# The last three output tiles: two copy engines and three DMA queues in place of one of each

## The chip, the cores and the metric

The kernel runs on one core of one Trainium2 chip. The metric is the device time of one execution in microseconds (us). A core has a matrix engine (PE, with PEld for its weight loads), a vector engine (DVE), a scalar engine (ACT), a general engine (POOL, called `gpsimd` in the code) and a queue engine (SP, `sync` in the code). SP, ACT and POOL can each start a DMA transfer. Each engine works through its own list of instructions in order; engines wait for one another by counting semaphores.

## The reference

Three layers run one after the other on 2304 tokens of 512 features.

```
ret  = (scale * q @ k^T) * decay_mask @ v            # 4 batches x 8 heads, 576 positions
x    = ret as (2304, 512)
x    = sum over the top 2 of 8 experts: weight * relu(x @ w1[e]) @ w2[e]
h    = x @ w_in                                      # (2304, 512) @ (512, 2048)
g    = h * clip(h + 3, 0, 6) / 6
out  = g @ w_out                                     # (2304, 512)
```

The change stands at the very end of the last product: where finished tiles of `out` leave the chip's on-core memory.

## The kernel before

Everything is float32; a product of the expert layers and of the last layer is made of three passes over high and low parts. `run` (L966) calls `attention`, `moe`, `moe2` and `rest` in that order.

`moe2` takes the 18 row tiles of 128 tokens in seven groups (`GR`): three groups of two tiles, then four of three. For each group, 16 steps of the hidden dimension (f = 0 to 15) are made: `g1` (L639) fills a PSUM tile `ga` or `gb`, `glu` (L814 to L817) applies the activation on ACT and DVE, and `g2` (L650) adds this step's part to the group's accumulators, one PSUM tile `p` of 128x512 for each row tile. `g2` runs one step late, through `flush`: the products of step f stand behind the `g1` of step f+1, so that PE need not wait for the activation. In `g2` the accumulators are finished one after the other: in the last step all products of the first, then of the second, then of the third.

When a group's last step is flushed, `o_out` copies each accumulator from PSUM to a row tile `s` on ACT (L824) and sends it to `out` from SP's queue (L825). For all groups but the last, this lies beside the next group's products. The last group, tiles 15 to 17, has nothing behind it.

Behind `moe2` stands `rest` (L868 to L872). It is for an uneven routing of tokens: each engine loads a count that was stored in the tile `more` early in the program (at 147.0 us) (`values_load`, L870), and skips the body when the count is zero (the `If`, L871). With this input it is zero, so all five engines jump over `rest_body`:

```
        most = nc.values_load(self.more[0:1, 8:9], min_val=0, max_val=MORE)
        with tc.If(most > 0):
            self.rest_body()
```

Behind the jump each engine has a few semaphore instructions that stand under L871; POOL has there one `INC_SWDGE_SEM`, which sets the counts of its DMA queue. Then comes the end of the tile context, whose instructions carry L1010: SP waits in turn for the counts of all DMA queues and engines, POOL has a `DRAIN` without any wait, and then all engines meet in a barrier that POOL collects and releases.

Of the kernel before, what the change touches and what calls it, by code (L numbers as in the profile page):

```python
# [12 lines left out]
AF = mybir.ActivationFunctionType  # L13
# [6 lines left out]
NT = N // 128  # L20
# [12 lines left out]
P = 128  # L33
# [31 lines left out]
class K:  # L65
# [754 lines left out]
    def o_out(self, t0, acc):  # L820
        nc = self.nc
        for j, a in enumerate(acc):
            o = self.row([P, DM])
            nc.scalar.activation(o, a, AF.Copy)  # L824
            nc.sync.dma_start(self.out[(t0 + j) * P:(t0 + j + 1) * P, :], o)  # L825

    def count(self):
# [185 lines left out]
```

## Time and profile before

| what | value |
|---|---|
| time, median of 3 runs | 1013.08 us (1012.91 to 1014.62) |
| the profiled execution's own time | 1017.49 us |
| span of the profiled execution, first to last instruction | 1015.7 us |
| PE busy | 982.1 us, 97% of the span |
| ACT, DVE, POOL busy | 411.0, 524.1, 190.8 us |
| mean granted TensorE clock | 0.989 |

The profiled execution is a single one with the profiler on; its own time lies 4.4 us above the median of the runs, and its span 1.8 us below its own time. All times inside the program are counted from the span's start. The end of the span is the end of the last instruction of any engine.

### The profile page before, as it was taken

How to read it: one execution, taken by the hardware profiler on the slowest of the kernel's cores; microseconds unless marked ns; L12 is line 12 of the kernel's file. 1: busy time of each engine (PE TensorE's matmuls, PEld its weight loads, DVE VectorE, ACT ScalarE, POOL GpSimd, SP SyncE). 2: the span in 40 equal slices, each digit the busy share in tenths (PEclk: the TensorE clock that was granted, in tenths of full speed). 3: DMA queues.
4: the chain of work that ended last, by engine and by line, in shares of the span. 5: the costliest groups of instructions: out<-in, count | busy, mean ns of one | idle time of the engine just before them, and what ended most of it. 6: DMA issues, size and time to landing. Idle time of an engine off the chain costs nothing.

```text
span 1015.7 us, 16598 instructions
## 1 busy us (share of the span) xinstructions
PE 982.1 (97%) x6268; PEld 876.9 (86%) x6268; DVE 524.1 (52%) x1264; ACT 411.0 (40%) x845; POOL 190.8 (19%) x257
## 2 busy tenths in 40 slices
PE   7999798999999999999999999999999999999996
PEld 5888687989888898988898889999999999999995
DVE  4679563767675767767664366333423333233221
ACT  3557423544334343533433365433333333333322
POOL 0043352023322332332320113011010100000000
PEclk9999899999999999999999999999999999999999
DMA  9998637744757366474525553111010110000000
GB/s 179 226 287 237 208 145 234 262 153 129 244 160 246 120 225 192 128 241 153 192 74 168 159 180 120 49 32 52 22 42 21 53 42 1 32 1 1 32 1 34
DMA packets 130921, 128.97 MB, mean 127 GB/s; under 512 B 66065, under 2 KB 94993, under 8 KB 130833
## 3 DMA queue, kind: packets, MB, share of 16 engines
q1 hardware_dynamic: 124432, 106.85, 35.5%
q0 software_dynamic: 6400, 20.98, 6.1%
q8 instruction: 51, 0.84, 0.3%
q14 instruction: 38, 0.30, 0.1%
HBM read 92.80 MB, written 35.00 MB: 126 GB/s over the span
## 4 chain that ended last, share of the span: by engine, by line
PE 86%; DMA 7%; DVE 2%; SPq 1%; ACT 1%; POOL 1%; issue 1%; another core or an unknown queue 0%; DVEq 0%; POOLq 0%; ACTq 0%
PE p L650 37%; PE ga L639 20%; PE gb L639 18%; DMA yd<-s 3%; PE xp L612 2%; PE px L218 2%; PE sc L196 2%; PE px L208 1%; PE p L179 1%; DMA s<-in_moe_w_out_dram 1%; DMA s<-in_moe_w_in_dram 1%; SPq L161 1%; PE p L256 1%; PE p L241 1%; POOL xe L377 1%
## 5 line engine op out<-in xcount | busy, mean ns | idle before, releaser
L650 PE MATMUL p<-b,h 128*128 128x512 f32 (+1 forms) x1824 | 452.1, 393 | 0.0
L650 PEld LDWEIGHTS p<-b,h 128*128 128x128 f32 (+1 forms) x1824 | 330.7, 186 | 65.3 <-DVE h L817 0.3
L639 PE MATMUL ga<-x,b 128*128 128x360 f32 (+2 forms) x1344 | 235.0, 324 | 0.8 <-ACT x L613 0.8
L639 PEld LDWEIGHTS ga<-x,b 128*128 128x128 f32 x1344 | 217.7, 189 | 7.8 <-ACT x L613 1.0
L639 PE MATMUL gb<-x,b 128*128 128x384 f32 (+2 forms) x768 | 129.5, 317 | 0.0
L639 PEld LDWEIGHTS gb<-x,b 128*128 128x128 f32 x768 | 121.0, 188 | 4.0
L583 POOL TENSOR_TENSOR cvl<-cvl,cva 128x256 f32<-128x256 f32 x64 | 48.8, 762 | 258.0 <-ACT h L692 113.3
L542 DVE TENSOR_TENSOR b<-b,b 128x512 fp32r<-128x512 f32 x128 | 89.6, 737 | 12.1 <-ACT b L541 8.5
L639 PE MATMUL gb<-b,b 128*128 128x256 f32 x672 | 89.8, 283 | 0.0
L817 DVE SCALAR_TENSOR_TENSOR h<-h,h 128x384 fp32r<-128x384 f32 (+1 forms) x112 | 56.2, 501 | 61.1 <-ACT h L816 61.1
L639 PEld LDWEIGHTS gb<-b,b 128*128 128x128 f32 x672 | 87.2, 192 | 0.4
L757 POOL DMA_INDIRECT s<-yd,slotc x36 | 34.8, 968 | 262.7 <-DVE s L766 81.8
L816 ACT ACTIVATE h<-h 128x384 fp32r<-128x384 f32 (+1 forms) x112 | 53.6, 479 | 63.6 <-DVE h L815 62.1
L541 ACT ACTIVATE b<-b 128x512 fp32r<-128x512 f32 x128 | 74.5, 625 | 11.7 <-PE p L650 11.6
L815 DVE SCALAR_TENSOR_TENSOR h<-h,ga 128x384 f32<-128x384 f32 (+1 forms) x56 | 27.8, 497 | 94.3 <-ACT h L814 94.0
L815 DVE SCALAR_TENSOR_TENSOR h<-h,gb 128x384 f32<-128x384 f32 (+1 forms) x56 | 27.8, 497 | 93.4 <-ACT h L814 93.3
L814 ACT ACTIVATE h<-ga,three 128x384 f32<-128x384 f32 (+1 forms) x56 | 30.0, 535 | 97.9 <-PE ga L639 94.6
L814 ACT ACTIVATE h<-gb,three 128x384 f32<-128x384 f32 (+1 forms) x56 | 30.0, 536 | 87.9 <-PE gb L639 86.1
L692 ACT ACTIVATE h<-ga 128x360 fp32r<-128x360 f32 (+1 forms) x64 | 29.4, 459 | 73.1 <-PE ga L639 61.4
L584 POOL TENSOR_TENSOR cvl<-cvt,cvl 128x256 f32<-128x256 f32 x64 | 56.7, 885 | 5.0
L693 DVE SCALAR_TENSOR_TENSOR h<-gb,h 128x256 fp32r<-128x256 f32 (+1 forms) x64 | 27.7, 433 | 53.8 <-PE p L650 33.6
L692 ACT ACTIVATE h<-gb 128x256 fp32r<-128x256 f32 (+1 forms) x64 | 25.3, 395 | 67.5 <-PE gb L639 67.3
(134 smaller groups left out, 871.0 us busy)
## 6 DMA issues: line engine op xcount, KB each, us to landing
b<-in_moe_w_dram SPq DMA_DIRECT2D x64, 512.0 KB
s<-in_moe_w_in_dram SPq DMA_DIRECT2D x32, 256.0 KB
s<-in_moe_w_out_dram SPq DMA_DIRECT2D x32, 256.0 KB
s<-xe SPq DMA_DIRECT2D x24, 240.0 KB
yd<-s SPq DMA_DIRECT2D x24, 240.0 KB
out_dram<-s SPq DMA_DIRECT2D x18, 256.0 KB
b<-in_k_dram SPq DMA_DIRECT2D x16, 256.0 KB
b<-in_q_dram SPq DMA_DIRECT2D x16, 256.0 KB
```

The costliest lines, as they stand in the source:

```text
L541: self.nc.scalar.activation(h, a, AF.Copy)
L542: self.nc.vector.tensor_sub(l, a, h.bitcast(F32))
L583: nc.gpsimd.tensor_mul(lf, lf, a.bitcast(F32))
L584: nc.gpsimd.tensor_add(lf, t.bitcast(F32), lf)
L639: nc.tensor.matmul(p, a[:, k, f], b[:, k, :n], start=(i == 0), stop=(i == 11))
L650: nc.tensor.matmul(a[:R], x[:, c], y[:, fi, :], start=(first and i == 0), stop=(last and i == 2))
L692: nc.scalar.activation(hh, p, AF.Relu)
L757: nc.gpsimd.indirect_dma_start(out=r, out_offset=None, in_=self.yd[0:rows], in_offset=bass.IndirectOffsetOnAxis(ap=self.slotc[:, t, k:k + ...
L814: nc.scalar.activation(r, p, AF.Relu, bias=self.three)
L815: nc.vector.scalar_tensor_tensor(r, r, 6.0, p, op0=OP.min, op1=OP.mult)
L816: nc.scalar.activation(gh, r, AF.Copy, scale=1.0 / 6.0)
L817: nc.vector.scalar_tensor_tensor(gl, r, 1.0 / 6.0, gh.bitcast(F32), op0=OP.mult, op1=OP.subtract)
```

## The change

In the last group (`last`), the first and the third accumulator are copied by ACT as before and the second by DVE. The three sends are issued by SP, POOL and ACT in this order, where SP issued all three. All other groups keep ACT and SP.

```diff
         for j, a in enumerate(acc):
             o = self.row([P, DM])
-            nc.scalar.activation(o, a, AF.Copy)
-            nc.sync.dma_start(self.out[(t0 + j) * P:(t0 + j + 1) * P, :], o)
+            last = t0 + len(acc) == NT
+            if last and j == 1:
+                nc.vector.tensor_copy(o, a)
+            else:
+                nc.scalar.activation(o, a, AF.Copy)
+
+            q = (nc.sync, nc.gpsimd, nc.scalar)[j] if last else nc.sync
+            q.dma_start(self.out[(t0 + j) * P:(t0 + j + 1) * P, :], o)
```

The change adds six lines ahead of `rest`, so that L870, L871 and L1010 of before are L876, L877 and L1016 of after.

SP, the end of its list ahead of the skipped body: the last three sends of `out`, the load of the count, a check of its range (ISA), and the jump. Before:

```order
L825 DMA out_dram<-s_10527 128x512
L825 DMA out_dram<-s_10530 128x512
L825 DMA out_dram<-s_10533 128x512
L870 TENSOR_LOAD more
L870 ISA x2
L871 COMPARE_AND_BRANCH
L906 DMA sd<-slots 128x18x2
```

And now:

```order
L831 DMA out_dram<-s_10527 128x512
L876 TENSOR_LOAD more
L876 ISA x2
L877 COMPARE_AND_BRANCH
L912 DMA sd<-slots 128x18x2
```

Two sends have left SP's list (`L906`, or `L912`, is the first row of the skipped body). The count is now loaded behind the first send of the three, not behind the third.

POOL, the same place: its last rows before were gathers of tokens for the last group, issued long before the end of the program. Before:

```order
L757 DMA s_9721<-yd,slotc 128x512
L757 DMA s_9848<-yd,slotc 128x512
L757 DMA s_9850<-yd,slotc 128x512
L870 TENSOR_LOAD more
L871 COMPARE_AND_BRANCH
```

And now:

```order
L757 DMA s_9848<-yd,slotc 128x512
L757 DMA s_9850<-yd,slotc 128x512
L831 DMA out_dram<-s_10530 128x512
L876 TENSOR_LOAD more
L877 COMPARE_AND_BRANCH
```

The send of the second tile stands between POOL's last gather and its load of the count; the load, the jump and all that follows the jump on POOL are behind that send, which waits for DVE's copy. In the same way DVE has its copy ahead of its load of the count, and ACT has one copy less and a send of the third tile ahead of its own.

## Rows read from the trace of the kernel before

**Rows 1.** The page: busy PE, the clock in 40 slices, the ended chain by engine.

```profile
PE 982.1 (97%) x6268; PEld 876.9 (86%) x6268; DVE 524.1 (52%) x1264; ACT 411.0 (40%) x845; POOL 190.8 (19%) x257
PEclk9999899999999999999999999999999999999999
PE 86%; DMA 7%; DVE 2%; SPq 1%; ACT 1%; POOL 1%; issue 1%; another core or an unknown queue 0%; DVEq 0%; POOLq 0%; ACTq 0%
```

**Rows 2.** Four stretches: busy us (instructions) by engine, clock, DMA share, GB/s.

```profile
core 0: us, PE busy (x) PEld busy (x) DVE busy (x) ACT busy (x) POOL busy (x), PEclk, DMA share, GB/s
943.00:1003.00 60.00, 60.00 (x305) 54.80 (x304) 15.58 (x28) 16.15 (x30) 0.00 (x0) 1.00 0.04 14
1003.00:1007.30 4.30, 4.27 (x18) 2.85 (x17) 1.11 (x2) 2.30 (x4) 0.00 (x0) 1.00 0.03 6
1007.30:1015.70 8.40, 0.00 (x0) 0.00 (x0) 0.00 (x0) 0.60 (x1) 0.00 (x0) 0.73 0.28 100
```

**Rows 3.** Order of time, from 1005.5 us: start, length, engine, line.

```profile
1005.12 2.15 PE L650 MATMUL p<-b,h 128*128 128x512 f32 x8
...
1005.92 1.98 ACT L824 ACTIVATE s<-p 128x512 f32<-128x512 f32 x3 [1.19 <-PE p L650]
1006.54 2.54 SPq L825 DMA_DIRECT2D out_dram<-s  x3
```

**Rows 4.** L825, the last three sends: ns min/median/max, first and last start.

```profile
L825 SPq DMA_DIRECT2D out_dram<-s x3: 332/383/1367, 1006.5 to 1008.7; - x3
```

**Rows 5.** L870, L871 and L1010 on SP: the load, the jump, the closing waits.

```profile
L870 SPq TENSOR_LOAD <-more x1: 685/685/685, 1009.1 to 1009.1; - x1
...
L871 SPq COMPARE_BRANCH  x1: 50/50/50, 1010.2 to 1010.2; - x1
L871 SPq EVENT_SEMAPHORE  x9: 17/17/17, 1013.4 to 1014.0; - x9
...
L1010 SPq DRAIN  x3: 7/7/13, 1014.8 to 1015.1; - x3
```

**Rows 6.** L870 and L871 on ACT, DVE and PE's weight loader.

```profile
L870 ACTq TENSOR_LOAD <-more x1: 732/732/732, 1007.3 to 1007.3; - x1
L871 ACTq COMPARE_BRANCH  x1: 50/50/50, 1008.1 to 1008.1; - x1
L871 ACTq EVENT_SEMAPHORE  x2: 17/17/17, 1010.6 to 1010.7; - x2
...
L870 DVEq TENSOR_LOAD <-more x1: 546/546/546, 1004.8 to 1004.8; - x1
L871 DVEq COMPARE_BRANCH  x1: 72/72/72, 1005.4 to 1005.4; - x1
L871 DVEq EVENT_SEMAPHORE  x2: 21/21/21, 1008.5 to 1008.6; - x2
...
L871 PEldq COMPARE_BRANCH  x1: 3822/3822/3822, 1006.0 to 1006.0; - x1
```

**Rows 7.** L870, L871 and L1010 on POOL.

```profile
L870 POOLq TENSOR_LOAD <-more x1: 501/501/501, 832.0 to 832.0; - x1
L871 POOLq COMPARE_BRANCH  x1: 53/53/53, 832.6 to 832.6; - x1
L871 POOLq EVENT_SEMAPHORE  x3: 17/17/17, 835.4 to 835.6; - x3
L871 POOLq INC_SWDGE_SEM  x1: 1784/1784/1784, 835.7 to 835.7; - x1
L1010 POOLq DRAIN  x3: 44/107/6600, 837.5 to 1015.4; - x3
L1010 POOLq EVENT_SEMAPHORE  x4: 17/17/17, 1014.9 to 1015.6; - x4
```

**Rows 8.** L757, POOL's gathers from 828 us on; DMA in 831 to 836 us, 40 slices.

```profile
L757 POOL DMA_INDIRECT s<-yd,slotc x2: 944/944/944, 828.7 to 832.2; - x2
...
DMA  8976100000000000000000199573889200000000
```

**Rows 9.** POOL's drain at the program's start (L998).

```profile
L998 POOLq DRAIN  x1: 198/198/198, 0.3 to 0.3; - x1
```

**Rows 10.** Copies and products of one 128x512 float32 tile on DVE.

```profile
L198 DVE TENSOR_TENSOR b<-sc,cst x36: 678/682/692, 9.4 to 119.1; 128x512 f32<-128x512 f32 x36
L624 DVE TENSOR_SCALAR s<-s x40: 415/419/428, 122.7 to 558.3; 120x512 f32<-120x512 f32 x24, 128x512 f32<-128x512 f32 x16
```

**Rows 11.** DMA from 1010 to 1014 us in 40 slices of 0.1 us.

```profile
DMA  9999691111140200000000000000000000000002
```

## Prediction

> **What bounds the kernel now.** I read the page first. PE is busy for 97% of the span, the granted clock is full in nearly every slice, and the chain that ended last is PE for 86% [rows 1]. The reader is to see there that over the whole run PE sets the time, and then to put that aside: the change touches no product, and the only PE work beside it ends before it matters. The stretches show this. From 943 to 1003 us PE is busy without a gap; from 1007.3 us to the end of the span, 8.4 us, PE is not busy at all and ACT for 0.60 us [rows 2]. So 8.4 us at the end belong to neither products nor copies, and the change can only move what lies in them.
>
> The order of time shows what the compute engines still do: PE's last products end at 1007.3, ACT's three copies run from 1005.92 to 1007.90, SP issues three sends from 1006.54 to 1009.08 [rows 3]. The third copy starts when the third accumulator is done, at 1007.3, so ACT follows PE and isn't late. The rest of the tail is sequencer work that no busy share counts, so I read it line by line. SP issues the sends (0.33, 1.37 and 0.38 us for one) [rows 4], loads the count at 1009.1, jumps at 1010.2, executes its next instruction only at 1013.4, 3.2 us later, goes through its closing waits until 1014.9, and 0.8 us of barrier later the span ends at 1015.7 [rows 5, 7]. The gap behind the jump is on every engine: 2.5 us on ACT, 3.0 on DVE, 3.8 within the branch on PE [rows 6], 2.8 on POOL [rows 7]. SP comes to its jump last, so SP sets the end. The last packets of `out` have moved by 1011.4 [rows 11], before SP even begins to wait for their counts: the sends themselves don't set the end.
>
> POOL has done its whole ending 170 us earlier: count at 832.0, jump at 832.6, next instruction at 835.4, the queue's count set at 835.7 (1.78 us), and then a drain that starts at 837.5 and takes 6.6 us, until 844.1. From the count's load to the drain's end that is 12.1 us, all hidden now [rows 7].
>
> **The change, part by part.** The sums are made against the profiled execution (span 1015.7, own time 1017.49 us) and carried as a difference to the median of 1013.08, which lies 4.4 us below it.
>
> *ACT loses a copy (0.60 us) and gets a send.* The third copy waits for PE until 1007.3 either way, so the lost copy is worth nothing; the other engine's copy lies beside it. The send must wait for the copy's end at 1007.9. No ACT send is in the trace; by SP's rows it takes 0.33 to 1.37 us. I take 0.33. Behind it ACT needs 3.4 us from the load of its count to its last semaphore (1007.3 to 1010.7) [rows 6], which makes 1011.6, or 1012.7 with the long issue. SP's closing waits ask for ACT's count near their end, at about 1012.5, so the long issue is just at the edge and the short one hidden.
>
> *SP loses two sends.* Its first send ends at 1006.9; its load of the count then stands at 1006.9 in place of 1009.1. Everything behind it on SP comes 2.2 us sooner, its last wait at 1012.7 in place of 1014.9. The bounds of this gain: 2.2 us if nothing else is late, nothing if another engine arrives at the barrier at 1014.9 or later.
>
> *DVE gets a copy.* The second accumulator is ready near 1006.6, when ACT began its second copy. The nearest rows are a DVE product from PSUM, 0.68 us, and a DVE operation within on-core memory, 0.42 us [rows 10]; I take 0.7, since the first reads PSUM too. The copy ends at 1007.3. DVE's own ending takes 3.8 us from the load of its count to its last semaphore [rows 6]; it is over by about 1010.5 and hidden by SP.
>
> *POOL gets a send.* This is the term that decides. The send waits for DVE's copy, so POOL's sequencer stands there until 1007.3, and the load of the count, the jump, `INC_SWDGE_SEM` and the drain are all queued behind it in POOL's list. The issue itself costs no more than before: in the trace POOL's last gather (0.94 us, from 832.2) [rows 8] runs while the load and the jump already go on beside it [rows 7], so I start the 12.1 us at 1007.3. That gives: jump at 1007.9, next instruction 1010.7, drain from 1012.8 to 1019.4. [...] The data of POOL's send is not in this sum: the packets of the last gather had moved by 835.0 [rows 8], 2.8 us after its issue, so POOL's send is in by about 1010.5.
>
> The unknown is the length of the drain. Rows give it between 0.04 us and 6.6 us: two POOL drains at the very end take 0.04 and 0.11 us [rows 7], one at the program's start 0.20 us [rows 9], and the one in just this place, behind the gathers and `INC_SWDGE_SEM`, 6.6 us. The change leaves its place and what stands ahead of it in the list alike, and adds one more transfer of POOL's kind, so I take 6.6. Nor was it waiting for data: the last packets were 2.5 us past when it began [rows 8]. With the lower bound the drain ends at 1013.0 and the span at 1013.8, **−1.9 us**. The jump on POOL may take longer than 2.8 us, since now all five engines jump within some 2 us: up to PE's 3.8, which adds up to 1.0.
>
> On the route of a send, the row has SP's issues at 2.5 us in all, of which 2.2 go. The Trainium skill (DMA: Bandwidth & Descriptors, "Issuing engines are not separate DMA queues") says that starting DMAs on several engines saves only the time that the sequencer takes to initiate them. By this page alone the sum would be −2.2 us; by the rows it is −2.2 on SP and +6.7 (1019.4 against 1012.7) on POOL. The same page ("SWDGE vs HWDGE vs iDMA") advises that plain transfers go to SP or ACT, without a price; the trace of before has no plain one on POOL.
>
> **The rivals.** *A: the drain is short* (0.2 us). Then POOL is ready at 1013.0, SP at 1012.7, and the span is 1.9 us shorter: 1011.2. For it: every other drain of POOL is that short, and the long one may belong to the busy stretch around 840 us rather than to its place. Against it: it is the only drain that has DMA work ahead of it. The point that decides is a drain of 2.1 us: from there POOL is at the barrier no sooner than SP was at 1014.9, and the gain is gone; from 4.1 us on the kernel is slower by more than 0.2%. The Trainium skill's sentence on several engines, above, would lead to nearly this time.
>
> *B: the drain is there, but partly paid off*, ending between 1014 and 1017: 1012 to 1015, no change that can be told. That needs a drain of 1 to 4 us, of which no row has an example.
>
> *C: POOL is later still*: a first plain send on POOL costs more than a gather, or the jumps hinder one another for more than the 1.0 us allowed above: 1019 to 1020. Against it: POOL's jump at 832.6 already was one of a program in full work.
>
> **How the numbers follow.** Forecast (drain of 6.6 us): 0.62; A: 0.20; B: 0.12; C: 0.06. The predicted time is 1013.08 + 4.5 = **1017.6 us**. The forecast's own range is 1016.6 to 1019.0, from the spread of the runs before (1012.91 to 1014.62) and the 1.0 us of the jump. The range that holds eight in ten has to take in A, so it goes from 1011.0 to 1019.3. A difference of 0.2%, 2.0 us, is about what a measurement can tell here. Slower takes the forecast, C and some of B: 0.69. Same takes A, whose −1.9 us is just short of the bound, and most of B: 0.27. Faster is left with the edge of A: 0.04.
>
> **What the changed profile would show.** The load of the count on SP at 1006.9 and SP's last closing wait at about 1012.7; DVE's copy of 0.7 us from 1006.6; on POOL the count's load at about 1007.3, the jump 0.6 us later, a drain that begins near 1012.8 and ends near 1019.4; the barrier behind it and nothing else busy. The span would be 1020.2. I'm wrong if POOL's drain there is under 4 us, or if the end is set by an engine other than POOL; everything ahead of 1005 us should stand as it was.

## The result, and the profile after

The changed kernel takes 1021.7 us (median of 7 runs, 1020.01 to 1028.44), the kernel before 1014.38 us (7 runs, 1012.91 to 1016.67). The ratio is 1.008, with a 95% interval of 1.0057 to 1.0102: slower by 6 to 10 us. The direction was forecast, the size was not: 1017.6 us was predicted, with a range up to 1019.3.

The profiled execution has a span of 1022.3 us against 1015.7, 6.6 us longer. All but 0.1 us of it lies behind the last product. The order of time from 1005.5 us on (start, length, engine, line; in brackets the idle time ahead of it and what ended it) answers to [rows 3]:

```profile
1005.27 2.12 PE L650 MATMUL p<-b,h 128*128 128x512 f32 x8
...
1006.06 0.60 ACT L828 ACTIVATE s<-p 128x512 f32<-128x512 f32 x1 [1.18 <-PE p L650]
1006.68 0.33 SPq L831 DMA_DIRECT2D out_dram<-s  x1
1006.75 0.69 DVE L826 COPY s<-p 128x512 f32<-128x512 f32 x1 [1.28 <-PE p L650]
1007.43 0.60 ACT L828 ACTIVATE s<-p 128x512 f32<-128x512 f32 x1 [0.78 <-PE p L650]
1007.74 0.60 POOL L831 DMA_DIRECT2D out_dram<-s  x1 [174.42 <-DVE s L826]
1008.06 0.38 ACTq L831 DMA_DIRECT2D out_dram<-s  x1
```

The copies and sends do what the change says, each on its engine, and the last send is issued at 1008.4 in place of 1009.1. PE's products end some 0.1 us later than before, which is no effect of the change. POOL had stood idle for 174 us until DVE's copy released it; that bracket is the change in one number.

What follows on POOL answers to [rows 7], line by line (lines 876, 877 and 1016 are 870, 871 and 1010 of before):

```profile
L876 POOLq TENSOR_LOAD <-more x1: 522/522/522, 1007.7 to 1007.7; - x1
L877 POOLq COMPARE_BRANCH  x1: 53/53/53, 1008.3 to 1008.3; - x1
L877 POOLq EVENT_SEMAPHORE  x3: 17/17/17, 1012.6 to 1012.8; - x3
L877 POOLq INC_SWDGE_SEM  x1: 1813/1813/1813, 1012.9 to 1012.9; - x1
L1016 POOLq DRAIN  x3: 44/113/6690, 1014.8 to 1022.0; - x3
L1016 POOLq EVENT_SEMAPHORE  x4: 17/17/17, 1021.5 to 1022.2; - x4
```

SP answers to [rows 5]:

```profile
L876 SPq TENSOR_LOAD <-more x1: 523/523/523, 1007.1 to 1007.1; - x1
L877 SPq COMPARE_BRANCH  x1: 50/50/50, 1008.0 to 1008.0; - x1
L877 SPq EVENT_SEMAPHORE  x9: 17/17/17, 1010.8 to 1012.5; - x9
L1016 SPq EVENT_SEMAPHORE  x14: 17/28/2016, 1012.6 to 1022.2; - x14
L1016 SPq DRAIN  x3: 7/7/13, 1015.3 to 1021.7; - x3
```

SP has its count 2.0 us sooner, as the change makes it. That gain is lost again. SP's nine semaphore instructions behind the jump take 1.7 us from first to last, where they took 0.6 before; why is not shown. One of its closing waits lasts 2.0 us (the 2016 ns), over a count of POOL's queue that POOL's `INC_SWDGE_SEM` sets only at 1014.7: this wait ends 0.06 us ahead of that instruction's end here and in e2, e7 and e10 below. SP is through at 1015.4, and stands 6 us more for POOL's drain.

### The profile page after: what moved, and what is told of

Same layout as the page of the kernel before. It is cut to its first block, busy times and chain, and to the rows that moved or that the text cites. A ratio compares the mean times of both kernels' runs of the same rounds, so it can differ in the third digit from the quotient of the medians.

```text
span 1022.3 us, 16598 instructions
## 1 busy us (share of the span) xinstructions
PE 981.6 (96%) x6268; PEld 876.5 (86%) x6268; DVE 525.7 (51%) x1265; ACT 410.6 (40%) x844; POOL 192.0 (19%) x258
## 4 chain that ended last, share of the span: by engine, by line
PE 66%; issue 21%; DMA 6%; DVE 2%; POOL 1%; SPq 1%; ACT 1%; POOLq 0%; DVEq 0%; ACTq 0%
PE p L650 27%; PE ga L639 16%; PE gb L639 13%; PE xp L612 2%; DMA s<-in_moe_w_out_dram 2%; PE px L218 2%; DMA s<-xe 1%; PE px L208 1%; PE sc L196 1%; DMA yd<-s 1%; PE p L179 1%; SPq L161 1%; PE p L256 1%; PE p L241 1%; POOL xe L377 1%
## 5 line engine op out<-in xcount | busy, mean ns | idle before, releaser
L757 POOL DMA_INDIRECT s<-yd,slotc x36 | 35.0, 971 | 262.6 <-DVE s L766 81.8
```

Source lines behind the costliest of these rows:

```text
L757: nc.gpsimd.indirect_dma_start(out=r, out_offset=None, in_=self.yd[0:rows], in_offset=bass.IndirectOffsetOnAxis(ap=self.slotc[:, t, k:k + ...
```

## The experiments

Theory P: the loss is POOL's ending, which the send moves from 832 us to behind the last tiles. Theory Q: sending from several queues costs, and POOL's drain only fills a wait. All ratios are to the kernel before, run on the same chip beside them (its medians there were 1009.1 to 1009.3 us). "Tail" is the time from the start of the last product to the end of the span: 8.83 us before, 15.28 us in the changed kernel. It leaves out the spread of the work ahead of it. But each tail comes from one execution: e4 below, whose last group does the same as the kernel before, has 8.00 us, so a difference of under 1 us between two tails tells nothing.

**e1_no_pool**, the changed kernel without its POOL send:

```diff
-            q = (nc.sync, nc.gpsimd, nc.scalar)[j] if last else nc.sync
+            q = (nc.sync, nc.sync, nc.scalar)[j] if last else nc.sync
```

> The changed kernel with its second send moved from POOL to SP; copies and ACT's send stay. Theory P (the loss is POOL's ending, moved behind the last tiles): the whole loss goes. SP's second send is issued near 1007.5 us and takes 0.33 to 1.37 us, its count's load stands near 1008 in place of 1009.1, so the span ends 0.3 to 1.3 us earlier than before: ratio to before 0.998 to 1.000. Theory Q (the loss comes from sending from several queues, ACT's first send or transfers that meet, and POOL's long drain only fills the wait): still slower by 3 us or more, ratio 1.003 and up.

Measured: ratio 0.9992 (0.998 to 1.0004), tail 8.46 us. The loss is gone, with DVE's copy and ACT's send still there. That is what P forecast; Q falls.

**e2_pool_alone**, the kernel before with one POOL send:

```diff
-            nc.sync.dma_start(self.out[(t0 + j) * P:(t0 + j + 1) * P, :], o)
+            q = nc.gpsimd if t0 + j == NT - 2 else nc.sync
+            q.dma_start(self.out[(t0 + j) * P:(t0 + j + 1) * P, :], o)
```

> The kernel before, with only the second of its last three sends moved from SP to POOL; all copies on ACT. Theory P: the same loss as the whole change. POOL is released near 1007.3 us by ACT's second copy, its drain starts between 1012.8 and 1014.8 and takes 6.6 us, and the span is 4.5 to 7 us longer: ratio 1.0045 to 1.007. Theory Q: without ACT's send and DVE's copy less than half of it, under 3 us.

Measured: ratio 1.0059 (1.0042 to 1.0076), tail 15.72 us. The POOL send alone makes the whole loss.

**e3_pool_touch**, one POOL instruction on one element, no POOL send:

```diff
             nc.sync.dma_start(self.out[(t0 + j) * P:(t0 + j + 1) * P, :], o)
+            if t0 + j == NT - 2:
+                nc.gpsimd.tensor_copy(self.spacer, o[0:1, 0:1])
```

> The kernel before, with one added POOL instruction and no POOL send: POOL copies one element of the second of the last three tiles once ACT has copied it, into a tile that nothing reads. Theory P1 (the drain of 6.6 us belongs to POOL's ending, whatever stood ahead of it): POOL's ending moves behind 1007.3 us as in the changed kernel, drain of about 6.6 us, 4.5 to 6.5 us slower, ratio 1.0045 to 1.0065. Theory P2 (the drain waits for a DMA that POOL issued some us ahead of it): the last gather is then 170 us past, the drain takes 0.2 us or less, POOL meets the barrier near 1013 to 1014.5, before SP, and the time is that of before within 0.2%.

Measured: ratio 1.0061 (1.0042 to 1.0081), tail 13.76 us. So it need not be a send: a copy of one element on POOL is enough. POOL's lines there (its copy is over at 1000.5 us):

```profile
L873 POOLq COMPARE_BRANCH  x1: 53/53/53, 1001.2 to 1001.2; - x1
L873 POOLq EVENT_SEMAPHORE  x3: 17/17/17, 1004.2 to 1004.4; - x3
L873 POOLq INC_SWDGE_SEM  x1: 1772/1772/1772, 1004.5 to 1004.5; - x1
...
L1012 POOLq DRAIN  x3: 44/107/6600, 1006.3 to 1013.4; - x3
```

The last gather of POOL had landed 178 us before, and the drain still takes 6.60 us. P2, that it waits for a transfer, falls.

**e4_pool_early**, a POOL send in the last group but one (as e2, with `NT - 5`):

> The kernel before, with one send moved to POOL, but in the last group but one (tiles 12 to 14, its second tile, near 943 us); the last three sends stay on SP. Theories P1 and P2: POOL's ending moves to 943 to 957 us, with its drain of about 6.6 us, and is hidden by 50 us of the last group's work: the same time as before within 0.2%. A rival, that a plain send from POOL is dear in itself wherever it stands (descriptors written by POOL, a queue that it shares with the gathers): slower by more than 2 us here too.

Measured: ratio 0.9992 (0.9979 to 1.0004), tail 8.00 us. The send is there, the ending with its drain of 6.69 us stands at 942.5 us beside 57 us of products, and costs nothing:

```profile
L1011 POOLq DRAIN  x3: 44/113/6690, 942.5 to 1007.3; - x3
```

**e5_act_two**, the three sends on SP, ACT and ACT:

```diff
-            q = (nc.sync, nc.gpsimd, nc.scalar)[j] if last else nc.sync
+            q = (nc.sync, nc.scalar, nc.scalar)[j] if last else nc.sync
```

> The changed kernel with its second send moved from POOL to ACT, so that SP sends one tile, ACT two, POOL none. Theory P (POOL's ending was the whole loss and SP's list sets the end otherwise): SP's load of the count stands 2.2 us sooner than before, as in the changed kernel, ACT's ending at about 5.7 us after the last matmul's start is just hidden, the tail from the last matmul's start to the end shrinks from 8.8 to 6.6 to 7.2 us: ratio 0.9978 to 0.9985. Rival: ACT's two sends make ACT the last at the barrier, and nothing is gained: ratio 0.9995 or more.

Measured: 1007.39 us against 1009.28, ratio 0.9982 (0.9973 to 0.9992), tail 6.86 us. This version is faster than the kernel before, and by the two ratios than the changed kernel too. SP's lines show why: the count at 1000.7 us, 0.05 us after the last product's start (2.26 before), and the last closing wait 6.0 us after it (8.0 before). Of this, 0.7 us are a wait for ACT's count (the 685 ns): the wait that the rival named is there, but too short to take the gain.

```profile
L876 SPq TENSOR_LOAD <-more x1: 519/519/519, 1000.7 to 1000.7; - x1
...
L1016 SPq EVENT_SEMAPHORE  x14: 17/28/685, 1005.2 to 1007.4; - x14
L1016 SPq DRAIN  x3: 7/7/13, 1006.6 to 1006.9; - x3
```

**e7_pool_late**, the changed kernel with POOL delayed:

```diff
+            if last and j == 1:
+                z = self.row([P, DM])
+                for _ in range(4):
+                    nc.gpsimd.tensor_copy(z, o)
             q.dma_start(self.out[(t0 + j) * P:(t0 + j + 1) * P, :], o)
```

> The changed kernel, with four copies of the second output tile on POOL (into a tile that nothing reads) ahead of POOL's send, so that POOL jumps some us after the other four engines. Theory J1 (POOL's jump took 4.3 us in the changed kernel and 2.9 before because all engines fetch code then): 2.6 to 3.4 us here, and the drain again 6.6 to 6.7 us. Theory J2 (a send of its own in flight makes POOL's jump long): 4 us or more here too. The time itself is longer than the changed kernel's by the copies, some 3 to 6 us.

Measured, in a single execution (1016.67 us, too few for a ratio): the drain 6.69 us, tail 16.53 us, and POOL's jump:

```profile
L881 POOLq COMPARE_BRANCH  x1: 53/53/53, 1001.7 to 1001.7; - x1
L881 POOLq EVENT_SEMAPHORE  x3: 17/17/17, 1005.2 to 1005.4; - x3
```

That is 3.5 us, between what J1 and J2 gave. The copies took 0.6 us each, less than I had reckoned, so POOL jumps only 1.4 us after ACT and the engines are not quite apart.

**e8_before_no_rest** and **e9_after_no_rest**, both kernels without the overflow path:

```diff
             self.moe2()
-            self.rest()
```

> The kernel before without the call of its overflow path behind the last layer (left out: the load of the count, the jump and the body that this input skips). Theory: SP goes from its third send, over at 2.2 us after the last matmul's start, straight to its closing waits and stands there until the third send's data are in, near 4.8 us; with 0.8 us of barrier the tail is about 6 us in place of 8.8, ratio 0.997. POOL's drain, now without INC_SWDGE_SEM ahead of it, tells whether that instruction makes it long: 6.6 us if it belongs to the end of the program, 0.2 us or less if it belongs to INC_SWDGE_SEM.

> The changed kernel without the overflow path (left out as in the run before it). If the drain of 6.6 us belongs to the end of the program: it starts within 1 us of POOL's send, near 1.5 us after the last matmul's start, ends near 8.1, tail about 9 us, so 3 us slower than the kernel before without that path and near the unshortened kernel before, ratio 0.999 to 1.001. If it belongs to INC_SWDGE_SEM: the drain is short, the tail about 5.5 us, ratio 0.9965.

Measured: e8 0.9964 (0.9952 to 0.9975), tail 4.25 us; e9 1.0011 (1.0001 to 1.0021), tail 8.82 us. The load of the count and the jump cost the kernel before 4.6 us of tail, more than I had taken (2.8); by the ratio it is 3.6 us. Some of it lies in the sends: SP's are over 1.4 us after the last product's start, 2.2 before, since the second takes 0.33 us here and took 1.37, and the last of SP's waits for their data ends 3.1 us after it, where I had taken 4.8. Why the second send is shorter is not shown. Between e8 and e9 there are 4.6 us of tail, again POOL's drain. It stands here without `INC_SWDGE_SEM`; in e8, behind the last gather:

```profile
L1009 POOLq DRAIN  x3: 40/102/7783, 825.0 to 1003.9; - x3
```

And in e9, behind the send:

```profile
L1015 POOLq DRAIN  x3: 40/108/7328, 999.4 to 1007.2; - x3
```

These records begin as the gather or the send ahead of them is taken up; counted from the end of that one, the drain is again 6.6 to 6.7 us. So it doesn't belong to `INC_SWDGE_SEM`.

**e10_early_drain_send**, the changed kernel with one drain more on POOL, behind its last gather:

```diff
                 self.x2_prep(gi + 1, f - 1)
+                if gi == len(self.GR) - 1 and f == 4:
+                    self.nc.gpsimd.drain()
```

> The changed kernel with one added POOL drain behind the last gather, near 833 us, hidden by the last group's products. Theory D1 (the long drain clears something that has piled up since the program's start, and only the first drain behind much work is long): the added drain takes 6.6 us, the closing one 0.2 us or less, POOL meets the barrier near 7.9 us after the last matmul's start, and the time is near that of before, ratio 0.999 to 1.001. Theory D2 (a POOL send or INC_SWDGE_SEM just ahead makes a drain long): the closing drain takes 6.6 us again, ratio 1.006 to 1.008, like the changed kernel.

Measured: 1008.75 us, ratio 0.9996 (0.9983 to 1.001), tail 7.51 us. The loss is gone with the POOL send still in place:

```profile
L808 POOLq DRAIN  x1: 7782/7782/7782, 824.3 to 824.3; - x1
...
L879 POOLq COMPARE_BRANCH  x1: 58/58/58, 1000.5 to 1000.5; - x1
L879 POOLq EVENT_SEMAPHORE  x3: 17/17/17, 1004.7 to 1004.9; - x3
L879 POOLq INC_SWDGE_SEM  x1: 203/203/203, 1005.0 to 1005.0; - x1
...
L1018 POOLq DRAIN  x3: 50/113/141, 1005.2 to 1006.4; - x3
```

The added drain at 824.3 us took the 6.6 us (and 1.2 us beside the gather), hidden by products. The closing one, in the same place behind the send and `INC_SWDGE_SEM`, takes 0.14 us, and `INC_SWDGE_SEM` 0.20 us in place of 1.81.

**e11_early_drain_touch**, the same drain added to e3:

> The kernel before with POOL's copy of one element of the last tile but one, no POOL send, and the added POOL drain behind the last gather. D1: the closing drain takes 0.2 us or less, time as before, ratio 0.999 to 1.001. D2 in its part on INC_SWDGE_SEM: the closing drain takes 6.6 us, ratio 1.0045 to 1.0065; if only a send makes it long, 0.2 us here and 6.6 us in the run with the send. A third, D3: a POOL drain takes 6.6 us at each place but right behind another one or at the program's start; then it is 6.6 us in both runs, as in D2.

Measured: ratio 1.0011 (0.9996 to 1.0026), tail 8.18 us, and the longest closing drain 0.107 us:

```profile
L875 POOLq INC_SWDGE_SEM  x1: 167/167/167, 1005.6 to 1005.6; - x1
...
L1014 POOLq DRAIN  x3: 38/41/107, 1005.8 to 1008.8; - x3
```

What D1 forecast came in both, and D2 and D3 fall: the drain is long only where much POOL work has passed since the last one. The lengths of the drains say more about what piles up. POOL issues 80 transfers in the kernel before:

```profile
xe<-s,slots POOLq DMA_INDIRECT x36
s<-yd,slotc POOLq DMA_INDIRECT x36
...
xe<-s,free POOLq DMA_INDIRECT x8
```

Behind these 80 the drain takes 6.60 us, also with e3's copy added. Behind 80 and a plain send it takes 6.69 us (the changed kernel, e2, e4, and e7 with its four copies). With e10's early drain only the one send lies ahead of the closing drain, 0.141 us, and in e11 only a copy, 0.041 us. So a send adds 0.09 to 0.10 us wherever it stands and copies add nothing, and 6.56 us over 80 transfers are 0.082 us for each. This last figure is an estimate: no run has another number of gathers, and what POOL's other work of those 800 us adds is not told apart.

**e6_copies_only**, the changed kernel's copies with `q = nc.sync`:

> The changed kernel's copies (ACT, DVE, ACT) with all three sends on SP. The third copy starts when the third accumulator is ready, as before, and SP's second send when the second copy is, some 0.1 us later since DVE's copy takes 0.69 us against 0.60: no change within 0.1%, ratio 0.999 to 1.001. A rival, that freeing ACT of one copy shortens the tail: 0.6 us, ratio 0.9994, which this measurement can hardly tell; the tail in the trace can.

Measured: ratio 1.0 (0.9986 to 1.0014), tail 9.08 us. The split of the copies alone gains nothing.

## Why the prediction was right in its mechanism and wrong in its size

**POOL gets a send, and its whole ending stands behind it.** Right. SP, ACT and DVE are through by 1015.4, 1012.3 and 1010.8 us, and POOL's drain ends at 1021.5. e1, e2 and e4 show that the POOL send at the end is the cause, and the only one.

**The drain takes 6.6 us again, not 0.2.** Right: 6.69 us, and rival A, a short drain, did not come. Rival B, a drain of 1 to 4 us, did not come either. Of the reason I gave, that its place and what stands ahead of it stay alike, only the second half holds: in e10 the drain has the same place and takes 0.14 us. What it is can be said better now: it is the first drain after POOL's work, and its length goes with the transfers that POOL has issued since the last one. The three short drains that I had as a lower bound [rows 7, 9] fit this: one comes at the program's start, ahead of all transfers, and two come behind a long one.

**POOL's ending takes 12.1 us from 1007.3.** This is the term that was mis-sized. It took 13.7 us (1007.7 to 1021.5), and began 0.4 us late. Nearly all of the 1.6 us is the jump: 4.3 us, where 2.8 were taken and 3.8 allowed. The bound of 1.0 us was PE's jump of 3.8, and no reason was given why POOL's should stay within it. Rival C, at 0.06, allowed for a jump longer by more than 1.0 us, and that came (1.5); its other half, that a plain send costs more to issue than a gather, did not (0.60 us against 0.94). Over the runs POOL's jump, from the branch's end to the next instruction, was:

| POOL's instruction just ahead | no other engine's jump beside it, or little | the other engines' jumps beside it |
|---|---|---|
| a gather | 2.5 to 2.8 (before, e1, e5, e6) | no run |
| a copy of one element | no run | 3.0 (e3), 3.2 (e11) |
| a plain send | 3.3 (e4), 3.5 (e7) | 4.3 (changed), 4.7 (e2), 4.2 (e10) |

Each number is from one profiled execution. The three of over 4 us have both, a send just ahead and the others' jumps beside them. But more of the others' jumps lies beside these three (8.4 to 9.7 us, added up over the four engines) than beside those of e3 and e11 (5.5 and 5.7 us), so how much the send does and how much the other jumps do is not told apart: J1 and J2 both stay open. The Trainium skill (Runtime: NRT & Kernel Launch, "Instruction fetch mechanics") says that a taken branch to a target outside the two pages at hand stalls until a DMA has fetched it. The trace agrees as far as it goes: POOL stands 2.5 to 4.7 us for one jump; in the kernel before, a packet of a queue called `instruction`, 8 KB, begins at 833.8 us, between POOL's jump (832.6) and its next instruction (835.4); and in e8, where nothing jumps, no such packet moves from 997 to 1004 us.

With +0.4, +1.6 and some 0.1 the sum of +4.5 becomes the 6.6 us of the trace. The interval of the ratio takes in 6.6 us.

**The sum was put on a median of three runs.** 1013.08 us rose to 1014.38 with seven. These 1.3 us and the 2.1 us of the trace make 3.4 of the 4.1 us between forecast and result; the rest is within the spread of the runs. The range, up to 1019.3, had too little: the trace's 2.1 us alone make 1019.7, and its upper end was made of a jump of 3.8 us and the spread that three runs had shown.

**SP comes 2.2 us sooner.** Right for its load of the count (2.0 us). But its last wait was forecast at 1012.7 and came at 1015.3: I had missed that SP waits for a count that POOL's `INC_SWDGE_SEM` sets (2.0 us). So rival A's 1011.2 us was too hopeful as well: with a short drain in e10 the tail is 1.3 us shorter than before, not 1.9, and the time is that of before (0.9996).

**The gain on SP is real where POOL is left out.** e5 has it: 1.9 us. The sentence of the Trainium skill (DMA: Bandwidth & Descriptors, "Issuing engines are not separate DMA queues") that only the sequencer's time is saved agrees with e5: two sends off SP's list are worth what SP spent on them. It says nothing of what follows on the engine that gets the send, which decided here.

**DVE's copy 0.7 us, ACT's send 0.33 us, the copies' split worth nothing.** Right: 0.69 us, 0.38 us, and e6.

## What to carry to other kernels

Ahead of giving an idle engine one last task, read what that engine still has to do behind it: here a load, a jump and a drain of 12 to 14 us, long done and hidden, came with a 0.6 us send. Move the late sends to an engine whose ending is short (ACT in e5, a gain of 1.9 us), or let the engine do its long drain early, under other work (e10, where the loss is gone but nothing gained). A row far from the end of the trace can be the most costly one there, once something moves it.

## What the runs showed of the hardware

- The first drain on POOL behind its work takes 6.6 to 6.7 us, with a transfer of POOL's in flight (e9), 178 us after the last one landed (e3), with and without `INC_SWDGE_SEM` (e9). A second one behind it takes 0.04 to 0.14 us, even with a new POOL send between them (e10). One more plain send makes a drain 0.09 to 0.10 us longer (6.60 and 6.69, 0.041 and 0.141), copies do not (e3, e7); for the 80 gathers and scatters here that makes an estimate of 0.082 us each. `INC_SWDGE_SEM` falls in the same way, from 1.8 us to 0.20 behind one send (e10) and 0.17 behind none (e11). What the drain does in this time stays open, and so does how long it is in a program where POOL has sent nothing.
- A plain send of a 128x512 tile took POOL 0.60 us to issue (0.94 for a gather), ACT 0.38, and SP 0.33 for the first of the last group; SP's second took 1.37 us in the kernel before and 0.33 in e8.
- A skipped `If` behind the last product is not free: without it the tail is 4.6 us shorter, and the ratio 0.9964 (e8).
